# One dummy matmul becomes 21 short ones, and the written-out orders change: a two-layer linear-attention and MLP kernel

## The chip, the core and the metric

The kernel runs on one core of a Trainium2 chip. The metric is the device time of one execution in microseconds (us), the median of some runs. A core has TensorE (PE, matmuls; its weight loads are listed as PEld), VectorE (DVE), ScalarE (ACT), GpSimd (POOL) and SyncE (SP, which issues most transfers), and 16 DMA engines that all queues share.

## The reference

x has 2048 tokens of 512 values in bfloat16. Two layers run the same two blocks, with the same weights.

```
x = x + A(layernorm(x));  x = x + B(layernorm(x))      # twice
A: q, k, v = y @ wqkv, 32 heads of 16
   phi(t) = where(t > 0, t + 1, exp(t)) + 1e-6
   kv = sum over tokens of phi(k) v^T;  z = sum over tokens of phi(k)
   out = (phi(q) kv) / (phi(q) z + 1e-6) @ wo
B: gelu(layernorm(y) @ w1 + b1) @ w2 + b2              # 512 -> 1792 -> 512
```

## The kernel before

**Tiles.** Tokens come in 16 tiles of 128 (named st, 0 to 15), four to a chunk (c, 0 to 3; k is the tile within it). Every step of work on a tile is one named operation, and most are one instruction. PE's operations are groups of matmuls: four of 512 columns accumulate over the 512 inputs.

**Names.** The first digit behind the letters is the layer (0 or 1).
- Loads: x0 and x1 (first chunk of x, tile 0 and tiles 1 to 3), xc1 to xc3 (the other chunks), wka to wkd (quarters of the key weights), wq, and later wv, wo, w1, w2.
- Layernorm of a tile (`norm`, line 757): stats (L775, DVE), aggr (L777), veps (L782, POOL or DVE), pow (the reciprocal root, L784, POOL), nmr (L795, POOL, only where ACT normalises), norm (L803 on DVE, L798 on ACT). The letter A or B behind a name tells the block. Tile 3 of layer 0 takes its sums on ACT (sumA0_3, sqA0_3).
- Transposes of normalised tiles: TA, TB, and TP for phi(q), as DMA transposes issued by SP one after the other (`transpose`, L812); PTA and PTC for the first four tiles by PE (`transpose_pe`, L825), with a copy tc on ACT (L835). Tiles 0 and 1 are transposed centred only (cenA0_0, cenA0_1), and the scale is put in later.
- Attention: K (L879) and Q (L896, L909) are projections; exp and relu on ACT and min and phi on DVE or POOL make phi of them (L847 to L864); G (L984, L1013) gathers y^T phi(k) over all tokens; Z (L970), ZH and za add up z, with zs sums on DVE; KV (L1034) and M (L1057) turn G into one matrix, through the copies cpg and cpm; D (L1100), ln, rec, pr or pz, red, den, rec, pr divide by the denominator; WO (L1123) multiplies and RA (L1128) adds to x.
- MLP: W1 (L1153) with a gelu on ACT for each (L1158), W2 (L1190, L1176) with RB (L1196, L1200); the last number of W1 is the token half where the first chunk is split; b2 adds the bias row to x. OD writes the output.

**Stages.** Chunk loads and K, G, Q of layer 0 (about 5 to 48 us), attention output and MLP of layer 0 chunk by chunk, with K, G and Q of layer 1 between (to about 200 us), then the same output and MLP of layer 1.

**Dummies.** `warm` (L749) is a group of PE matmuls on a constant whose result nobody reads. `WARM` in CONF lists the columns of each; warm0 has seven matmuls of 512 columns, warm1 to warm8 one of 256 each. Each matmul has its own weight load.

**What sets the order.** `CONF` holds it, written out: `ORDER` lists for each engine its operations in sequence, `PLACES` which buffer each tile uses, `WAY` which engine runs an operation that can go to several. At build time the operations are issued in exactly this order, and `assign_waits` puts a semaphore wait before an instruction wherever its data or its buffer depends on another engine. An engine doesn't pass a waiting instruction. The numbers of expected durations in the code only decide ties of this writing out; no planner runs in the kernel.

The heads of PE's and DVE's lists are these (PE's list begins at line 254):

```
pe:  warm0 warm8 warm2 warm6 PTC0 warm1 warm7 warm5 warm4 warm3 K0_0a K0_0b PTC1 K0_0c K0_0d PTA0_2 K0_1 PTA0_3 K0_2
     K0_3 G0_0_0 G0_1_0 Q0_0_2 Q0_0_1 Q0_0_0 K0_5 G0_2_0 K0_4 Z0_0 G0_3_0 Q0_1_0 K0_7 Q0_1_3 K0_6 ...
dve: ones statsA0_0 aggrA0_0 cenA0_0 statsA0_2 statsA0_1 aggrA0_2 aggrA0_1 cenA0_1 normA0_0 vepsA0_1 normA0_2
     statsA0_5 normA0_3 aggrA0_5 normA0_1 statsA0_4 mink0_0 ...
```

Of the kernel before, what the change touches and what calls it, by code (L numbers as in the profile page):

```python
# [185 lines left out]
def assign_waits(graph, order, sems, dma_sems):  # L186
# [10 lines left out]
    while len(done) < total:  # L197
        moved = False
        for e in ENGINES:
# [42 lines left out]
    WARM=[[512, 512, 512, 512, 512, 512, 512], [256], [256], [256], [256], [256], [256], [256], [256]],  # L242
    LOADS=[['x0', 'sp', 'x', 0, 0, 1, ''], ['x1', 'sp', 'x', 0, 1, 4, ''], ['wkb', 'act', 'wk', 0, 2, 3, 'ones'], ['wka', 'sp', 'wk', 0, 0, 1, ''], ['wkd', 'act', 'wk', 0, 3, 4, ''], ['wkc', 'sp', 'wk', 0, 1, 2, ''], ['xc1', 'sp', 'x', 1, 0, 4, 'x0'], ['wq', 'sp', 'wq', 0, 0, 4, ''], ['xc3', 'sp', 'x', 3, 0, 4, ''], ['xc2', 'sp', 'x', 2, 0, 4, '']],
    ORDER={
# [39 lines left out]
        "act":  # L284
# [324 lines left out]
def build_kernel(nc, A_x, A_wqkv, A_wo, B_x, B_w1, B_b1, B_w2, B_b2, out, conf=None, report=False):  # L609
# [5 lines left out]
    with ExitStack() as es:  # L615
# [137 lines left out]
        def by_token(L, c):  # L753
            return eng(f"den{L}_{c}") == "tok"
# [605 lines left out]
```

## Time and profile before

| | |
|---|---|
| median of 3 runs | 323.07 us (322.53 to 324.76) |
| profiled execution, its time | 323.1 us |
| its span, first to last instruction | 321.9 us |
| busy: PE, DVE, ACT, POOL | 318.0, 218.1, 189.3, 145.5 us |
| matmuls (each with a weight load) | 1703 |
| instruction packets, queues q8 and q14 | 13 (0.21 MB) and 10 (0.08 MB) |

How to read it: in rows of the timeline and of the chain, the first number is the start and the second the length, in us; then the engine, the line of the kernel, what is written and read, and how often. A bracket gives the engine's idle time ahead of it and what ended it. A row of the waits gives engine, output and line, what it waited for, us in total, times, and the longest. A matmul's length in the trace has a tail of some 0.16 us that overlaps with the next; the distance of starts tells the pace. A matmul of 512 columns follows the one before by 0.216 us for most of the run.

### The profile page before, as it was taken

To read this page: it belongs to the slowest core of one execution; us is meant where nothing else is said; L and a number is where in the kernel's file an instruction comes from. 1 tells how busy PE (TensorE), PEld (TensorE's weight loads), DVE (VectorE), ACT (ScalarE), POOL (GpSimd) and SP (SyncE) were. 2 spreads that over 40 slices of the span, in tenths; PEclk is the share of its full clock that TensorE was granted. 3 is DMA by queue.
4 is the path that set the end of the run, shared out by engine and by line. 5 is a ranking of instruction groups with operands and counts; after the bars stand their busy time and mean duration, and the time that the engine had idled before them with its cause. 6 is when DMAs were issued, how large, how long until landed. Compare 5 with 4: busy or idle time off the path is not lost.

```text
span 321.9 us, 4748 instructions
## 1 busy us (share of the span) xinstructions
PE 318.0 (99%) x1703; PEld 157.4 (49%) x1703; DVE 218.1 (68%) x529; ACT 189.3 (59%) x324; POOL 145.5 (45%) x216
## 2 busy tenths in 40 slices
PE   8999999999999999999999999999999999999997
PEld 3444554666444444444444444558544444444444
DVE  5998789999786774028848899999889881101103
ACT  5898656797730636667962367979634442663320
POOL 6573978688655355101822415887454163000000
DMA  7844793142121412111010200122232322201002
GB/s 257 200 81 85 241 348 85 35 82 36 33 49 34 82 33 51 34 33 32 18 40 10 51 16 0 35 51 52 50 62 54 98 65 67 49 0 35 16 33 65
DMA packets 52355, 21.68 MB, mean 67 GB/s; under 512 B 47532, under 2 KB 50860, under 8 KB 52332
## 3 DMA queue, kind: packets, MB, share of 16 engines
q1 hardware_dynamic: 50844, 16.37, 22.4%
q0 software_dynamic: 1056, 4.72, 4.3%
q10 hardware_dynamic: 432, 0.30, 0.3%
q8 instruction: 13, 0.21, 0.3%
q14 instruction: 10, 0.08, 0.1%
HBM read 8.00 MB, written 2.10 MB: 31 GB/s over the span
## 4 chain that ended last, share of the span: by engine, by line
PE 97%; DMA 2%; DVE 0%; issue 0%
PE ps L1153 30%; PE ps L1190 29%; PE ps L1123 9%; PE ps L879 8%; PE ps L896 6%; PE ps L984 4%; PE ps L1013 4%; DMA t<-in_A_x_dram 2%; PE ps L909 2%; PE ps L1176 1%; PE ps L970 1%; PE ps L1034 1%; PE ps L1057 1%; PE ps L1100 1%; DVE stats L775 0%; PE ps L1048 0%
## 5 line engine op out<-in xcount | busy, mean ns | idle before, releaser
L1158 ACT ACTIVATE gT<-ps,b1c 128x512 bf16<-128x512 f32 (+1 forms) x140 | 77.0, 601 | 68.7 <-PE ps L1153 68.1
L1153 PE MATMUL ps<-t,w 128*128 128x512 bf16 (+1 forms) x560 | 102.5, 336 | 0.0
L1190 PE MATMUL ps<-w,gT 128*128 128x512 bf16 x434 | 98.6, 379 | 0.0
L1153 PEld LDWEIGHTS ps<-t,w 128*128 128x128 bf16 x560 | 54.8, 98 | 43.7 <-ACT gT L1158 0.2
L1190 PEld LDWEIGHTS ps<-w,gT 128*128 128x128 bf16 x434 | 42.5, 98 | 50.4
L784 POOL TENSOR_TENSOR rstd<-veps,neghalf 128x1 f32<-128x1 f32 x64 | 39.0, 625 | 41.1 <-DVE veps L782 38.9
L847 ACT ACTIVATE eb<-ps 128x512 bf16<-128x512 f32 x62 | 35.4, 606 | 19.3 <-PE ps L896 7.3
L1200 DVE TENSOR_TENSOR yb<-ps,xsb 128x512 bf16<-128x512 f32 x15 | 10.2, 688 | 41.4 <-PE ps L1190 41.4
L775 DVE BATCH_NORM_STATS2 stats<-xsb 128x6 f32<-128x512 f32 x48 | 32.0, 681 | 0.3
L1123 PE MATMUL ps<-gtb,t 128*128 128x512 bf16 x128 | 31.4, 379 | 0.0
L879 PE MATMUL ps<-wqkv,t 128*128 128x512 bf16 x128 | 30.9, 379 | 0.3 <-ACT t L835 0.3
L858 ACT ACTIVATE rb<-ps 128x512 bf16<-128x512 f32 x43 | 25.3, 607 | 5.8 <-PE ps L879 5.8
L798 ACT ACTIVATE yb<-xsb,nmr,rstd 128x512 bf16<-128x512 f32 x21 | 16.9, 814 | 15.1 <-POOL nmr L795 15.1
L896 PE MATMUL ps<-wqkv,t 128*128 128x512 bf16 x96 | 24.1, 379 | 0.0
L1089 POOL TENSOR_TENSOR t<-t,rr 128x512 bf16<-128x512 bf16 x18 | 19.3, 1072 | 9.0 <-DVE rr L1085 6.4
L782 POOL TENSOR_SCALAR veps<-mv 128x1 f32<-128x1 f32 x35 | 8.2, 236 | 32.7 <-DVE mv L777 31.3
L1196 DVE TENSOR_TENSOR xsb<-ps,xsb 128x512 f32<-128x512 f32 x16 | 10.8, 678 | 17.9 <-PE ps L1190 17.9
L1139 POOL TENSOR_TENSOR xsb<-xsb,b2b 128x512 f32<-128x512 f32 x17 | 21.4, 1267 | 3.0 <-DVE yb L803 2.9
L1077 POOL TENSOR_TENSOR lr<-t,zrow 128x512 f32<-128x512 bf16 x14 | 16.5, 1179 | 7.3 <-ACT zrow L997 4.5
L1123 PEld LDWEIGHTS ps<-gtb,t 128*128 128x128 bf16 x128 | 12.5, 98 | 14.5
L803 DVE TENSOR_SCALAR yb<-xsb,mv,rstd 128x512 bf16<-128x512 f32 x27 | 14.5, 542 | 7.3 <-POOL rstd L784 6.0
L879 PEld LDWEIGHTS ps<-wqkv,t 128*128 128x128 bf16 x128 | 12.1, 98 | 14.7 <-ACT t L835 0.9
(99 smaller groups left out, 363.7 us busy)
## 6 DMA issues: line engine op xcount, KB each, us to landing
w<-in_B_w_dram POOLq DMA_DIRECT2D x4, 896.0 KB, 9.1
out_dram<-yb SPq DMA_DIRECT2D x15, 128.0 KB, 2.0
t<-in_A_x_dram SPq DMA_DIRECT2D x3, 512.0 KB, 4.8
t<-yb SPq DMA_TRANSPOSE x62, 2.5
wqkv<-in_A_wqkv_dram SPq DMA_DIRECT2D x1, 512.0 KB, 5.9
wqkv<-in_A_wqkv_dram POOLq DMA_DIRECT2D x1, 512.0 KB, 4.7
wo<-in_A_wo_dram POOLq DMA_DIRECT2D x1, 512.0 KB, 5.3
t<-in_A_x_dram SPq DMA_DIRECT2D x1, 384.0 KB, 3.3
```

The source lines that it names most:

```text
L775: G.op("dve", lambda e: e.bn_stats(stats[:, s.slot, :], src()), 620, reads=src_keys, writes=[k + "s"], tiles=[s, *src_tiles], name=f"stats ...
L784: G.op("pool", lambda e: e.tensor_tensor(rstd[:, s.slot:s.slot + 1], veps[:, s.slot:s.slot + 1], neghalf[:], op=ALU.pow), 570, reads=[k + ...
L847: G.op("act", lambda e: e.activation(eb[:, et.slot, :], bank(bt), ACT.Exp, scale=by()), 478, reads=[src_key, *more_keys], writes=[f"e{tag} ...
L858: G.op("act", lambda e: e.activation(rb[:, rt.slot, :], bank(bt), ACT.Relu, scale=by()), 478, reads=[src_key, *more_keys], writes=[f"r{tag ...
L879: ins = e.matmul(bank(b), lhsT=yTa(yT)[:, dt, k * P:(k + 1) * P], rhs=wqkv[:, dt, D:2 * D], start=(i == 0 and n == 0), stop=(i == len(part ...
L896: ins = e.matmul(bank(b), lhsT=yTa(yT)[:, dt, k * P:(k + 1) * P], rhs=wqkv[:, dt, 0:D], start=(dt == 0), stop=(dt == DT - 1))
L1089: lambda e, d=d, tok=tok, heads=heads: e.tensor_tensor(heads(tok()), heads(tok()), rr[:, d.slot, :].unsqueeze(2).broadcast_to([P, H, DH]), ...
L1123: ins = e.matmul(bank(wb), lhsT=yTa(pq)[:, kt, k * P:(k + 1) * P], rhs=gtb[:, kt, :], start=(kt == 0), stop=(kt == DT - 1))
L1139: G.op("pool" if on_pool else "dve", lambda e: e.tensor_tensor(xsb[:, st, :], xsb[:, st, :], b2b[:], op=ALU.add), 1120 if on_pool else 600 ...
L1153: ins = e.matmul(bank(b, n), lhsT=w1[:, dt, ft * P:(ft + 1) * P], rhs=yTa(yT)[:, dt, k0 * P:k1 * P], start=(dt == 0), stop=(dt == DT - 1))
L1158: G.op("act", lambda e, ft=ft, b=b, k0=k0, k1=k1, n=n: e.activation(gT[:, g.slot, ft * 512 + k0 * P:ft * 512 + k1 * P], bank(b, n), ACT.Ge ...
L1190: ins = e.matmul(bank(b), lhsT=gT[:, g.slot, ft * 512 + k * P:ft * 512 + (k + 1) * P], rhs=w2[:, ft, :], start=(ft == 0), stop=(ft == FT - 1))
```

## The change

It has three parts.

1. The seventh matmul of warm0 (512 columns) becomes 21 of 24 columns each. PE then has 1723 matmuls. The other eight dummies stay, but only warm5 and warm6 come ahead of PTC0, and six behind it.
2. `ORDER`, `PLACES` and `WAY` are written anew. The lists of loads and the first 16 entries of SP stay as they are; most other lists are permuted, from place to place, up to about the second chunk of the last MLP.
3. The code gets options: an order of chunks for each phase (`CHUNKS`), a load of half a tile, and a "half" way for the denominator, in which two tiles of a chunk go one way and two the other. `CHUNKS` names 0 to 3 in order, and neither `LOADS` nor `WAY` names a half.

```diff
-    WARM=[[512, 512, 512, 512, 512, 512, 512], [256], [256], [256], [256], [256], [256], [256], [256]],
+    WARM=[[512, 512, 512, 512, 512, 512, 24, 24, 24, 24, 24, 24, 24, 24, 24, 24, 24, 24, 24, 24, 24, 24, 24, 24, 24, 24, 24], [256], [256], [256], [256], [256], [256], [256], [256]],
+    CHUNKS=[[0, 1, 2, 3], [0, 1, 2, 3], [0, 1, 2, 3]],
...
         "pe":
-            "warm0 warm8 warm2 warm6 PTC0 warm1 warm7 warm5 warm4 warm3 K0_0a K0_0b PTC1 K0_0c K0_0d PTA0_2 K0_1 PTA0_3 K0_2 "
-            "K0_3 G0_0_0 G0_1_0 Q0_0_2 Q0_0_1 Q0_0_0 K0_5 G0_2_0 K0_4 Z0_0 G0_3_0 Q0_1_0 K0_7 Q0_1_3 K0_6 G0_4_0 G0_5_0 "
+            "warm0 warm5 warm6 PTC0 warm8 warm1 warm3 warm4 warm2 warm7 K0_0a K0_0b K0_0c PTC1 K0_0d PTA0_2 K0_1 PTA0_3 K0_2 "
+            "K0_3 G0_0_0 G0_1_0 Q0_0_2 Q0_0_1 Q0_0_0 K0_5 G0_2_0 G0_3_0 K0_4 Q0_1_0 K0_7 Q0_1_3 Z0_0 G0_4_0 K0_6 G0_5_0 "
...
-            "W11_0_8_0 W11_0_2_0 W11_0_7_0 W11_0_1_0 W11_0_0_0 W11_0_10_0 W11_0_4_0 W11_0_9_0 W11_0_13_0 W11_0_5_0 W11_0_3_0 "
-            "W11_0_0_1 W11_0_12_1 ...
+            "W11_0_9_0 W11_0_13_0 W11_0_8_0 W11_0_7_0 W11_0_4_0 W11_0_2_0 W11_0_1_0 W11_0_12_0 W11_0_0_0 W11_0_5_0 W11_0_13_1 "
+            "W11_0_5_1 W11_0_12_1 W11_0_10_0 W11_0_10_1 ...
         "dve":
-            "ones statsA0_0 aggrA0_0 cenA0_0 statsA0_2 statsA0_1 aggrA0_2 aggrA0_1 cenA0_1 normA0_0 vepsA0_1 normA0_2 "
-            "statsA0_5 normA0_3 aggrA0_5 normA0_1 statsA0_4 mink0_0 aggrA0_4 phik0_0 mink0_1 normA0_5 phik0_1 statsA0_7 "
-            "normA0_4 aggrA0_7 mink0_2 statsA0_13 mink0_3 statsA0_6 aggrA0_13 minq0_0_2 statsA0_14 aggrA0_6 phik0_2 "
-            "statsA0_12 phik0_3 statsA0_8 normA0_6 ...
+            "ones statsA0_0 aggrA0_0 vepsA0_0 cenA0_0 statsA0_2 statsA0_1 aggrA0_2 aggrA0_1 cenA0_1 normA0_0 vepsA0_1 "
+            "normA0_2 statsA0_5 normA0_3 normA0_1 aggrA0_5 statsA0_4 mink0_0 aggrA0_4 phik0_0 mink0_1 normA0_5 phik0_1 "
+            "statsA0_7 normA0_4 aggrA0_7 statsA0_6 statsA0_12 mink0_3 statsA0_13 mink0_2 aggrA0_6 aggrA0_13 phik0_2 aggrA0_12 "
+            "statsA0_15 phik0_3 aggrA0_15 statsA0_14 minq0_0_2 mink0_5 aggrA0_14 normA0_6 ...
         "pool":
-            "id0 neghalf bdm0 bdm1 id1 vepsA0_0 powA0_0 ...
+            "id0 bdm0 b1z id1 neghalf powA0_0 ... nmrA0_10 eps6 powA0_11 bdm1 nmrA0_11 powA0_9 phik0_14 wv phik0_8 wo ...
...
     # WAY, what changes sides
-    b20_3, b20_4, b20_11, b20_13, b21_3, b21_4, pr0_0_1, pr1_2_2: pool
+    b20_3, b20_4, b20_11, b20_13, b21_3, b21_4, pr0_0_1, pr1_2_2: dve
-    b21_2, pr1_3_0, pz0_2_0, pz1_2_2, pz1_3_3: dve
+    b21_2, pr1_3_0, pz0_2_0, pz1_2_2, pz1_3_3: pool
     # and some veps and za, in both directions
...
-        def by_token(L, c):
-            return eng(f"den{L}_{c}") == "tok"
+        def by_token(L, c, k=0):
+            way = eng(f"den{L}_{c}")
+            return way == "tok" or (way == "half" and k >= 2)
+
+        def by_half(L, c):
+            return eng(f"den{L}_{c}") == "half"
...
-        for c in range(NC):
+        orders = cf["CHUNKS"]
+        for c in orders[0]:
```

More of the change, by code (lines that the diff above doesn't have):

```diff
@@ L709, in load_w, with load_half @@
                                [f"{which}_{d}" for d in range(d0, d1)], name=name, kb=128 * (d1 - d0), after=after)
+        def load_half(name, queue, h, after):
+            G.parts[("x0", 0)] = (("x0", 0, 0), ("x0", 0, 1))
+            ps_ = slice(64 * h, 64 * h + 64)
+            loaded[name] = dma(queue, lambda e: e.dma_start(
+                t4[ps_, x0[0].slot, 0:D].rearrange("p (k d) -> p k d", k=1), rows(x_dram, 0)[ps_, 0:1, :]),
+                [("x0", 0, h)], [x0[0]], name=name, kb=64, after=after)
         for name, queue, what, at, lo, hi, behind in cf["LOADS"]:
             after = [loaded[b] for b in behind.split()]
-            if what == "x":
+            if what == "half":
+                load_half(name, queue, at, after)
+            elif what == "x":
                 load_x(name, queue, at, lo, hi, after)
@@ L887, in attn_q, with fn @@
         def attn_q(L, c, yT, pq):
-            if by_token(L, c):
-                for k in range(4):
+            half = by_half(L, c)
+            own = pq
+            if half:
+                own = tokq[(L, c)] = Tile(T4, f"pqt{L}_{c}")
+            n = 2 * P if half else 4 * P
+            if not by_token(L, c):
+                for kt in range(DT):
+                    b = Tile(psum, f"q{L}_{c}_{kt}" + "c" * half, "q")
+                    def fn(e, kt=kt, b=b):
+                        for dt in range(DT):
+                            ins = e.matmul(bank(b, n), lhsT=wqkv[:, dt, kt * P:(kt + 1) * P], rhs=yTa(yT)[:, dt, 0:n],
+                                           start=(dt == 0), stop=(dt == DT - 1))
+                        return ins
+                    G.op("pe", fn, 4 * MM if n == D else 4 * (n / 2.4 + 2.5), reads=[f"yT{L}_{4 * c + k}" for k in range(n // P)] + ["wq"], writes=[f"q{L}_{c}_{kt}" + "c" * half],
+                         tiles=[b, yT], name=f"Q{L}_{c}_{kt}" + "c" * half, lat=MM_DRAIN, n=4)
+                    phi(b, f"q{L}_{c}_{kt}" + "c" * half, lambda kt=kt: yTa(pq)[:, kt, 0:n], f"pq{L}_{c}_{kt}" + "c" * half, [pq], f"q{L}_{c}_{kt}" + "c" * half, n=n)
+            for k in range(4):
+                if by_token(L, c, k):
                     b = Tile(psum, f"q{L}_{c}_{k}", "q")
@@ L900, in attn_q, with attn_z @@
                          tiles=[b, yT], name=f"Q{L}_{c}_{k}", lat=MM_DRAIN, n=4)
-                    phi(b, f"q{L}_{c}_{k}", lambda k=k: t4[:, pq.slot, k * D:(k + 1) * D], f"pq{L}_{c}_{k}", [pq],
+                    phi(b, f"q{L}_{c}_{k}", lambda k=k: t4[:, own.slot, k * D:(k + 1) * D], f"pq{L}_{c}_{k}", [own],
                         f"q{L}_{c}_{k}")
-                return
-            for kt in range(DT):
-                b = Tile(psum, f"q{L}_{c}_{kt}", "q")
-                def fn(e, kt=kt, b=b):
-                    for dt in range(DT):
-                        ins = e.matmul(bank(b), lhsT=wqkv[:, dt, kt * P:(kt + 1) * P], rhs=yTa(yT)[:, dt, :],
-                                       start=(dt == 0), stop=(dt == DT - 1))
-                    return ins
-                G.op("pe", fn, 4 * MM, reads=[f"yT{L}_{4 * c + k}" for k in range(4)] + ["wq"], writes=[f"q{L}_{c}_{kt}"],
-                     tiles=[b, yT], name=f"Q{L}_{c}_{kt}", lat=MM_DRAIN, n=4)
-                phi(b, f"q{L}_{c}_{kt}", lambda kt=kt: yTa(pq)[:, kt, :], f"pq{L}_{c}_{kt}", [pq], f"q{L}_{c}_{kt}")
         zfirst = {}
-        def attn_z(L, c, pks):
-            by_sum = [int(v) for v in (eng("zc0") or "").split()] if L == 0 else list(range(NC - 1))
+        def attn_z(L, c, pks, order):
+            by_sum = [int(v) for v in (eng("zc0") or "").split()] if L == 0 else order[:NC - 1]
+            others = [v for v in order if v not in by_sum]
             def fold(add):
@@ L973, in attn_z, with attn_g_held @@
             G.op("pe", fn, 400, reads=[f"pk{L}_{4 * c + k}" for k in range(4)] + ["onesm"], writes=[f"zc{L}_{c}"], tiles=[b, *pks], name=f"Z{L}_{c}", lat=MM_DRAIN, n=16)
-            total(b, f"zc{L}_{c}", f"zs{L}_{c}", bool(L) or c != min(v for v in range(NC) if v not in by_sum))
-            if L == 0 and by_sum and c == max(v for v in range(NC) if v not in by_sum):
+            total(b, f"zc{L}_{c}", f"zs{L}_{c}", bool(L) or c != others[0])
+            if L == 0 and by_sum and c == others[-1]:
                 fold(True)
-        def attn_g_held(L, st, k, y, ykey, pk, gb):
-            parts = [(dc,) for dc in range(DT)] if st == ST - 1 else [tuple(range(DT))]
+        def attn_g_held(L, st, k, y, ykey, pk, gb, first, last):
+            parts = [(dc,) for dc in range(DT)] if last else [tuple(range(DT))]
             for part in parts:
@@ L984, in fn @@
                         ins = e.matmul(ps[:, gb.slot + dc, :], lhsT=yb[:, y.slot, dc * P:(dc + 1) * P], rhs=pkb[:, pk.slot, :],
-                                       start=(st == 0), stop=(st == ST - 1))
+                                       start=first, stop=last)
                     return ins
                 keys = [f"g{L}_{dc}" for dc in part]
-                G.op("pe", fn, len(part) * MM, reads=[ykey, f"pk{L}_{st}"] + (keys if st else []), writes=keys,
+                G.op("pe", fn, len(part) * MM, reads=[ykey, f"pk{L}_{st}"] + ([] if first else keys), writes=keys,
                      tiles=[y, pk, gb], name=f"G{L}_{st}_{part[0]}", lat=MM_DRAIN, n=len(part))
@@ L1004, in attn_g_out, with attn_g_chunk @@
                 copy(gtb[:, dc, :], gb, f"g{L}_{dc}", ("gt", dc), dc % 2, f"g{L}_{dc}", off=dc)
-        def attn_g_chunk(L, c, ys, ykeys, pks):
+        def attn_g_chunk(L, c, ys, ykeys, pks, first, last):
             for dc in range(DT):
@@ L1042, in attn_kv @@
                  reads=["zs", "bdmask"], writes=["zb"], name=f"zb{L}", lat=40, fast=True)
-            if any(by_token(L, c) for c in range(NC)):
+            if any(by_token(L, c, 3) for c in range(NC)):
                 zr = Tile(psum, f"zr{L}", "t")
@@ new lines, in attn_den @@
+            half = by_half(L, c)
+            src = tokq[(L, c)] if half else pq
+            pt = pq if half or not by_token(L, c) else Tile(T4, f"pt{L}_{c}")
+            n = 2 * P if half else 4 * P
+            if not by_token(L, c):
+                for kt in range(DT):
+                    tag = f"{L}_{c}_{kt}" + "c" * half
+                    b = Tile(psum, f"d{tag}", "n")
+                    r = Tile(LR, f"lr{tag}")
+                    key = f"pq{L}_{c}_{kt}" + "c" * half
+                    G.op("pe", lambda e, kt=kt, b=b: e.matmul(bank(b, n), lhsT=zb[:, kt * P:(kt + 1) * P], rhs=yTa(pq)[:, kt, 0:n], start=True, stop=True),
+                         MM if n == D else n / 2.4 + 2.5, reads=[key, "zb"], writes=[f"d{tag}"], tiles=[b, pq], name=f"D{tag}", lat=MM_DRAIN)
+                    G.op("act", lambda e, b=b, r=r: e.activation(lr[:, r.slot, 0:n], bank(b, n), ACT.Ln, bias=eps6[:]), 575 if n == D else 362,
+                         reads=[f"d{tag}", "eps6"], writes=[f"l{tag}"], tiles=[b, r], name=f"ln{tag}", lat=90, table="exp")
+                    G.op("act", lambda e, r=r: e.activation(lr[:, r.slot, 0:n], lr[:, r.slot, 0:n], ACT.Exp, scale=-1.0), 536 if n == D else 323,
+                         reads=[f"l{tag}"], writes=[f"l{tag}"], tiles=[r], name=f"rec{tag}", lat=110, table="exp")
@@ L1093, in attn_den @@
[L1093 to L1105 removed]
+                         lambda e, kt=kt, r=r: e.tensor_tensor(yTa(pq)[:, kt, 0:n], yTa(pq)[:, kt, 0:n], lr[:, r.slot, 0:n], op=ALU.mult),
@@ new lines, in attn_den, with attn_out @@
+                     1150 if on_pool else 600, reads=[f"rr{tag}", f"pq{tag}"], writes=[f"pq{tag}"], tiles=[d, src],
+                     name=f"pr{tag}", lat=60, fast=not on_pool)
+                dma("sp", lambda e, k=k, tok=tok: e.dma_start_transpose(yTa(pt)[:, :, k * P:(k + 1) * P], tok()), [f"pt{tag}"],
+                    tiles=[src, pt], reads=[f"pq{tag}"], name=f"TP{tag}", sem=("pT", src, k), transpose=True)
+            return pt
+        def attn_out(L, c, k, pq, base, base_keys, base_tiles, first):
@@ L1116, in attn_out @@
             st = 4 * c + k
             wb = Tile(psum, f"wo{L}_{st}", "w")
-            parts = [(kt,) for kt in range(DT)] if st == 0 else [tuple(range(DT))]
+            parts = [(kt,) for kt in range(DT)] if first else [tuple(range(DT))]
             for part in parts:
@@ L1141, in mlp_front, with mlp_up @@
                  fast=not on_pool)
-        def mlp_up(L, c, yT, g):
-            parts = [(0, 2), (2, 4)] if c == 0 else [(0, 4)]
+        def mlp_up(L, c, yT, g, first):
+            parts = [(0, 2), (2, 4)] if first else [(0, 4)]
             for hf, (k0, k1) in enumerate(parts):
@@ L1252, in build_kernel @@
         for L in range(2):
-            nxt = []
-            for c in range(NC):
+            nxt = {}
+            chunks = orders[1 + L]
+            for c in chunks:
                 yT = Tile(T4, f"yBT{L}_{c}")
```

118 lines of the change are left out of this document (51 added, 67 removed), and 432 rows, old and new, of tables (ORDER, PLACES, WAY).

## The prediction

> **What bounds the kernel now.** I read the page's busy times first, then the chain that ended last, then the waits of TensorE (PE), then the first 12 us of the timeline.
>
> ```profile
> span 321.9 us, 4748 instructions
> PE 318.0 (99%) x1703; PEld 157.4 (49%) x1703; DVE 218.1 (68%) x529; ACT 189.3 (59%) x324; POOL 145.5 (45%) x216
> ...
> PE 97%; DMA 2%; DVE 0%; issue 0%
> ```
>
> PE is busy 318.0 of 321.9 us, and 97% of the chain is PE. The next view, PE's waits, holds every one of them; none is longer than 0.8 us:
>
> ```profile
> PE ps L749 <- PEq L1345: 0.8, 1, 0.8
> PE ps L825 <- DVE yb L803: 0.5, 1, 0.5
> PE ps L879 <- ACT t L835: 0.3, 1, 0.3
> PE ps L825 <- DVE yb L789: 0.2, 1, 0.2
> ```
>
> The chain's first rows and the timeline place these waits; all lie before 9.16 us.
>
> ```profile
> 3.24 4.83 DMA t<-in_A_x_dram
> ...
> 8.09 0.69 DVE stats L775
> 8.79 0.33 DVE yb L803
> ...
> 9.16 0.40 PE ps L825 x4
> 9.56 1.73 PE ps L879 x8
> ```
>
> The load xc1 (second chunk of x) is issued at 3.24 and lands at 8.07. VectorE (DVE) has statsA0_5, which needs it, ahead of normA0_3 in its order, so normA0_3 runs at 8.70 to 9.10, and PE starts PTA0_3 at 9.16. From there to its last matmul PE runs without a gap: 512-column matmuls follow each other every 1.73/8 = 0.216 us, and the table by windows gives PE 50.84 busy of 50.84 us from 9.16 to 60.00, and full stretches after it until 319.70. So two things can change the time: when PE gets past PTA0_3, and new gaps after it. There is no old gap after it to remove.
>
> **The sum's base.** The profiled execution took 323.1 us: span 321.9 and 1.2 around it. The median of the three timed runs is 323.07 (322.53 to 324.76), so the profiled one stands for the median. A measurement of this kernel tells about 1% (3.2 us) from no change.
>
> **The code parts.** CHUNKS lists 0 to 3 in order three times, no unit is marked "half", no load "half". The new branches then issue what the old ones did: cost 0, nothing hides it because nothing runs. The real matmuls (1688, 1703 less 15 dummies) stay the same in number and shape; the order names are permuted.
>
> **The dummies.** Before PTC0, PE has warm0 and three groups of 256; after it, five more. The weight loads' starts give the pace:
>
> ```profile
> 2.49 0.15 PEld L749 LDWEIGHTS ps<-const-bfloat16-1.0 128*128 128x128 bf16 x1 [0.28 <-issue]
> 2.91 0.15 PEld L749 LDWEIGHTS ps<-const-bfloat16-1.0 128*128 128x128 bf16 x1 [0.28 <-issue]
> ```
>
> A dummy of 512 columns takes 0.43 us here, twice the 0.216 of later; the 256s go at 0.214 until about 4.2 us, at 0.112 after PTC0. The seventh starts at 3.34. It becomes 21 of 24 columns. No row has 24 columns at the slow pace. Lower bound: 16 one-column matmuls of L970 take 0.38 us in the chain, 24 ns each, so 21 take 0.50. Upper bound: 128 columns at the slow pace, half of the 0.214 of a 256, is 0.107, so 21 take 2.25. I take twice the one-column row, 0.048, since it is the nearest: 1.01 us, against 0.43 removed: +0.58. One 256 moves behind PTC0: -0.21. So the dummies before PTC0 end at about 4.39 + 0.37 = 4.76 (bounds 4.25 and 6.0). PTC0's other condition, cenA0_0, now has vepsA0_0 ahead of it on DVE, 0.05 to 0.14 us (a L782 row on DVE lasts 0.14), so 4.6 to 4.7. PTC0 goes from 4.61 to about 4.76. ScalarE (ACT) reads it in tcC0 at 5.23, behind sumA0_3; PTC0 would end at 5.0 + 0.2, so nothing is lost. Six dummies of 0.112 follow until about 5.7, under K0_0a at 5.86. K0_0c moves ahead of PTC1; its weights wkd landed at 5.93, so it fits from 6.3 to 6.5, before PTC1 at 6.55. All of this ends before PTA0_3, which waits for xc1; LOADS and the first eleven entries of SP are unchanged. The slack: K0_1's last matmul streams until 8.53, 0.63 us before PTA0_3; on ACT expk0_0 ends at 9.22 and tcA0_3 starts at 9.59, 0.37. **Cost 0**; at the upper bound PTC0 is 1.4 late, less 0.63 to 0.37 of cover and 0.25 of moved dummies, some +0.5.
>
> The Trainium skill, "TensorE: Matmul & The Clock Gate", section "What's actually happening", says that a window of about 3.4 us of activity releases the array's clock from half rate, and that the window runs free of the kernel's start. The trace agrees in that the pace doubles 3.4 us after the first dummy at 0.83; by that rule alone the short ones change nothing if they count as activity, and the sum stays.
>
> **The instruction packets.** The page lists "q8 instruction" with 13 packets, in the trace 110 to 149 matmuls apart, so this queue brings PE's instructions. The first is at 18.05 us and takes 1.26 us. Twenty more matmuls ahead bring every later one 20 matmuls earlier: 20 x 0.216 = 4.3 us, so the first comes near 13.7. A packet costs PE nothing by itself (no gap at any of the 13). But look at the transposes' landings, page first, then the DMA view of 17 to 19 us:
>
> ```profile
> t<-yb SPq DMA_TRANSPOSE x62, 2.5
> ```
>
> ```profile
> q8 instruction: 1, 0.02, 3.9%
> issues: line engine op xcount, KB each, median us to landing
> t<-yb SPq DMA_TRANSPOSE x1, 4.1
> ```
>
> TA0_6, in flight beside the packet, took 4.05 us against 2.45: stretched by 1.6 us. It landed at 21.76, and K0_6 started at 21.89, so the stretch was just covered. Freeing TA0_6 therefore gains **0**: PE was not waiting. At 13.7 the packet meets the load xc2 (10.76 to 14.58) and TA0_5, queued behind it (11.45 to 15.14); K0_5 starts at 15.44, as it does in the new order: cover 0.29. Bounds: 0 (TA0_5's own packets run after 14.6, when a packet begun at 13.3 is through) and 1.6 - 0.29 = 1.3. PE's sequencer runs a varying distance ahead (the same 110 to 149), so the place is uncertain by a few us. I take 0, as most of TA0_5's flight is waiting for xc2, and keep 1.3.
>
> The skill, "Runtime: NRT & Kernel Launch", section "Instruction fetch mechanics", has fetch mostly hidden from the engine. By that the shift costs 0; for PE itself the trace agrees, for the transposes beside it TA0_6 does not.
>
> **The orders.** I follow the new ones by start-to-start steps of rows: a statistics 0.61 us on DVE, min 0.19, aggregate 0.09, normalise or bf16 sum 0.31, PE's groups of four 0.863. DVE's order is the old one up to aggrA0_7 at 12.71. Then statsA0_6 12.80, statsA0_12 13.41, mink0_3 14.02, statsA0_13 14.21, mink0_2 14.82, two aggregates, phik0_2 15.19, ending 15.59 (was 15.83; G0_2 is due at 16.30). Aggregate, statsA0_15, phik0_3 16.20 to 16.60; G0_3 has moved ahead of K0_4 to 17.16: cover 0.56. normA0_6 moves from 17.28 to 17.68, so TA0_6 lands at about 20.6, at 22.2 if stretched; K0_6 moves back to 22.73: cover 0.5 at least. Later tight places, in the same way: WO0_0_1 at 51.18 needs pr0_0_1, which moves from POOL to DVE behind cpm0_2 (there 49.6 to 50.3) and ends at 50.9: cover 0.2, was 0.78. W11_0_13_1, the first on the second token half in layer 1, comes 13 x 0.437 after 215.12, at 220.80; TB1_3 landed at 220.12: cover 0.68. Between 60 and 66 us and 217 and 223 us PE is 0.2 to 0.6 us behind the gelus that free its banks, as before, since the same matmuls and gelus alternate. bdm1 moves on POOL from 2.5 to about 25 us, 0.85 us, ahead of nmrA0_11; normA0_11 ran at 27.44, nmrA0_11 ended at 26.48: up to 0.1 left, then TA0_11's place in its queue at 28.93 still covers 0.6. Six b2 additions go from POOL to DVE and one back, three products with zrow from DVE to POOL: PE waits for none of them in the trace. The orders from about 248 us on are the same. **Cost 0**, with bounds of -0.5 (the lowest timed run is 0.5 under the median, so some stalls differ between executions) and +1.5 (the highest is 1.7 over).
>
> **Sum**: 323.1 + 0 + 0 + 0 = 323.1 us.
>
> **Rivals.**
> - **The packet lands on TA0_5 (slower).** Place: K0_5. Price 1.26, the packet's own time, less 0.29: 0.97, giving 324.1; 324.4 with the whole 1.6. It decides once TA0_5 lands after 15.38. For it: the stretch of TA0_6; against: TA0_5 mostly waits for xc2. Chance 0.27.
> - **Executions get steadier (faster).** Orders with wider covers (phik0_9 now ends 0.9 us before the matmul that needs its bank, Z0_2's 0.19 grows) save stalls that the profiled execution didn't have: 322.5, the lowest time. Against: the profiled execution has no such stall and takes the median. Chance 0.17.
> - **The start is late.** Slow dummies as in the upper bound, or the slow pace lasting one such stretch of 3.4 us longer, to 7.6: PTC0 from 4.8, six dummies at 0.214 to 6.6, K0_0a to K0_0c at 0.43 to 7.9, PTC1, then tcC1 and K0_1 until about 9.7, 0.5 after PTA0_3's data: 323.6. Against: the covers above, and the doubling in the trace at 4.2. Chance 0.08. (That the pace doubles at another moment in another execution is what the same page's section would have.)
> - **A stage falls out of step.** The gelu stages have 0.2 us of cover; DVE takes over POOL's work there. More than 3.2 us must come together: 327. Chance 0.05.
> - **The packets don't move**, because the sequencer waits elsewhere: 323.1, same as the forecast, counted in it.
>
> **How the numbers follow.** Forecast 0.43 (322.8 to 323.5). A gain of 1% is out of reach: PE's idle time from 4.60 to 9.16 is 4.56 less 2.4 us of real matmuls (eight of 0.216, twelve transposes of 0.058), 2.1 us in all, and xc1 pins it: faster 0.01. Slower by over 1% comes from the last stage case: 0.05. Within 1%: 0.94. The range takes in the steadier case with 0.3 for its own spread, and the packet case with the whole stretch and 0.3 more: 322.2 to 324.7.
>
> **What would show it.** PE's waits after 9.2 us: none by the forecast; one on L879 before 16 us by the packet rival. PTA0_3 near 9.16 and xc1 near 8.07. The first q8 packet near 13.7. TA0_6 landing in 2.5 us. The weight loads of L749 between 3.3 and 4.7 us give the short dummies' pace. I am wrong if a gap of PE appears at WO0_0_1, W11_0_13_1 or in the gelu stages.

## The result and the profile after

The changed kernel takes 324.41 us (median of 22 runs, 322.66 to 326.99); the kernel before takes 323.19 beside it (22 runs, 322.53 to 325.58). The ratio is 1.0038 with a 95% interval of 1.0024 to 1.0053: 1.2 us slower, inside the forecast's range and within 1%, but not the "no change" of 323.1. The profiled execution took 324.38 us, so it stands for the median.

The page of the changed kernel, busy times and chain:

```profile
span 323.1 us, 4750 instructions
PE 317.0 (98%) x1692; PEld 157.9 (49%) x1723; DVE 221.0 (68%) x534; ACT 189.8 (59%) x324; POOL 143.4 (44%) x211
...
PE 93%; DVE 3%; DMA 2%; issue 1%; ACT 1%
```

The trace lacks 31 matmul records (1692 of 1723 are there, all weight loads are), so a single step of 0.43 us between matmuls is a lost record here and no gap. DVE now holds 3% of the chain, where it held nothing. PE's waits show why:

```profile
PE ps L1151 <- DVE t L1104: 1.1, 1, 1.1
PE ps L761 <- PEq L1375: 0.8, 1, 0.8
PE ps L843 <- DVE yb L821: 0.3, 1, 0.3
PE ps L843 <- DVE yb L807: 0.2, 1, 0.2
```

The last three lie at the start, as all waits of the kernel before did (dummies, PTA0_2, PTC0). The first is new and is the longest of the kernel: L1151 is WO, L1104 the product pr. It is a gap after 9.16 us, which the kernel before didn't have. PE's timeline places it; a bracket holds the idle time ahead of the row:

```profile
50.98 0.38 PE L1151 MATMUL ps<-gtb,t 128*128 128x512 bf16 x1
52.45 0.82 PE L1151 MATMUL ps<-gtb,t 128*128 128x512 bf16 x3 [1.09 <-DVE t L1104]
```

WO0_0_0 starts at 50.98, WO0_0_1 at 52.45 instead of 51.20: 1.26 us lost. The rows of the chain that answer to those of the start:

```profile
3.27 4.55 DMA t<-in_A_x_dram
...
7.85 0.69 DVE stats L793
8.54 0.33 DVE yb L821
8.92 0.40 PE ps L843 x4
```

xc1 landed at 7.83 (8.07 before), and PTA0_3 starts at 8.92 (9.16): -0.24. A third difference lies at K0_5, 15.47, which is 6.55 us behind PTA0_3 where it was 6.28: +0.27. The profile puts this small gap down to ACT's exponential expq0_0_2, which ends at 15.45, because that came last. But K0_5's first weight load starts at 15.44, before that end, and in e2 below, with the same orders, K0_5 starts at 15.38, ahead of the end of expq0_0_2 at 15.63. What PE waited for is the transpose TA0_5: it landed at 15.33 (15.14 before), behind the load xc2, which landed at 14.77 (14.58 before). So what the start gained was lost again here.

Together 1.26 + 0.27 - 0.24 = 1.29, and the unrounded spans differ by 323.14 - 321.85 = 1.29. The whole difference of the two profiled executions is placed.

**What DVE did meanwhile.** First DVE, then POOL, in the changed kernel:

```profile
49.24 1.21 DVE L869 TENSOR_SCALAR eb<-eb 128x512 bf16<-128x512 bf16 x1
...
50.64 0.62 DVE L1023 TENSOR_SCALAR gtb<-ps 128x512 bf16<-128x512 f32 x1
51.18 1.21 DVE L1104 TENSOR_TENSOR t<-t,lr 128x512 bf16<-128x512 bf16 x1
```

```profile
49.25 1.05 POOL L1134 TENSOR_TENSOR t<-t,rr 128x512 bf16<-128x512 bf16 x1
50.79 1.05 POOL L1134 TENSOR_TENSOR t<-t,rr 128x512 bf16<-128x512 bf16 x1 [0.49 <-DVE rr L1130]
```

The row at 49.24 is minq0_2_0. It took 0.28 us in the kernel before:

```profile
50.36 0.28 DVE L851 TENSOR_SCALAR eb<-eb 128x512 bf16<-128x512 bf16 x1
```

In the changed kernel it starts within 0.01 us of POOL's product pr0_1_1 and ends at 50.45, 0.15 after that product ends at 50.30. The row at 51.18 is the moved pr0_0_1: it ends at 52.40, 0.55 after POOL's next product pr0_1_0 (50.79 to 51.85), though it needs some 0.68 in all. cpm0_2 between them, at 50.64, reads PSUM and runs beside POOL's product in 0.62. So these two DVE instructions, whose operands all lie in SBUF, stand still beside POOL's products: minq0_2_0 loses 0.93 us and pr0_0_1 0.53.

That matches a rule of the Trainium skill, "SBUF — State Buffer", section "SBUF: two separate sides": DVE and GpSimd share one pair of SBUF ports as an exclusive lock; a DVE instruction takes it when it runs in a 2-port performance mode or has two inputs in SBUF, the one that starts first keeps it for its whole instruction, and PE, ACT and DVE's own pair wait for nobody. The rows above agree for pr0_0_1, with its two SBUF inputs, and for the instruction with a PSUM source that isn't held up. minq0_2_0 has one input; that it runs in such a mode no trace here states.

From here on, the **toss** is the question which of minq0_2_0 (DVE) and pr0_1_1 (POOL) goes ahead and which is held up. Only their lengths tell it, not the starts in the rows: here DVE's row starts 0.01 us ahead of POOL's and is the one held up. They meet because the instructions ahead of both, den0_1_0 on DVE and pz0_1_2 on POOL, end together (49.33 and 49.29).

### The profile page after: what moved, and what is told of

Read it like the earlier page. It is cut to its first block, busy times and chain, and to the rows that moved or that the text cites. A ratio compares the mean times of both kernels' runs of the same rounds, so it can differ in the third digit from the quotient of the medians.

```text
span 323.1 us, 4750 instructions
## 1 busy us (share of the span) xinstructions
PE 317.0 (98%) x1692; PEld 157.9 (49%) x1723; DVE 221.0 (68%) x534; ACT 189.8 (59%) x324; POOL 143.4 (44%) x211
## 4 chain that ended last, share of the span: by engine, by line
PE 93%; DVE 3%; DMA 2%; issue 1%; ACT 1%
PE ps L1181 30%; PE ps L1218 29%; PE ps L1151 8%; PE ps L897 8%; PE ps L930 5%; PE ps L1036 4%; PE ps L1007 4%; DMA t<-in_A_x_dram 2%; PE ps L918 2%; PE ps L1204 1%; DVE gtb L1023 1%; PE ps L993 1%; DVE rd L1125 0%; DVE t L1104 0%; DVE eb L869 0%
## 5 line engine op out<-in xcount | busy, mean ns | idle before, releaser
L1181 PE MATMUL ps<-t,w 128*128 128x512 bf16 (+1 forms) x552 | 101.9, 336 | 0.4
L1181 PEld LDWEIGHTS ps<-t,w 128*128 128x128 bf16 x560 | 54.8, 98 | 43.7 <-ACT gT L1186 0.6
L802 POOL TENSOR_TENSOR rstd<-veps,neghalf 128x1 f32<-128x1 f32 x64 | 41.2, 659 | 23.1 <-DVE veps L800 21.3
L1151 PE MATMUL ps<-gtb,t 128*128 128x512 bf16 x124 | 31.3, 379 | 1.3 <-DVE t L1104 1.1
L897 PE MATMUL ps<-wqkv,t 128*128 128x512 bf16 x125 | 30.6, 379 | 0.3
L1122 POOL TENSOR_TENSOR lr<-t,zrow 128x512 f32<-128x512 bf16 x17 | 19.7, 1160 | 9.9 <-ACT zrow L1020 4.7
L1151 PEld LDWEIGHTS ps<-gtb,t 128*128 128x128 bf16 x128 | 12.4, 98 | 15.8 <-DVE t L1104 1.6
L897 PEld LDWEIGHTS ps<-wqkv,t 128*128 128x128 bf16 x128 | 12.2, 98 | 15.0 <-ACT t L853 0.6
L981 POOL TENSOR_TENSOR zacc<-zacc,pkb 128x512 f32<-128x512 f32 x5 | 6.2, 1243 | 28.9 <-DVE mv L795 19.6
L821 DVE TENSOR_SCALAR yb<-xsb,mv,rstd 128x512 bf16<-128x512 f32 x27 | 15.2, 568 | 3.2 <-POOL rstd L802 2.9
```

The source lines that it names most:

```text
L802: G.op("pool", lambda e: e.tensor_tensor(rstd[:, s.slot:s.slot + 1], veps[:, s.slot:s.slot + 1], neghalf[:], op=ALU.pow), 570, reads=[k + ...
L897: ins = e.matmul(bank(b), lhsT=yTa(yT)[:, dt, k * P:(k + 1) * P], rhs=wqkv[:, dt, D:2 * D], start=(i == 0 and n == 0), stop=(i == len(part ...
L1122: lambda e, r=r, tok=tok: e.tensor_tensor(lr[:, r.slot, :], tok(), zrow[:], op=ALU.mult), 1150 if on_pool else 600,
L1151: ins = e.matmul(bank(wb), lhsT=yTa(pq)[:, kt, k * P:(k + 1) * P], rhs=gtb[:, kt, :], start=(kt == 0), stop=(kt == DT - 1))
L1181: ins = e.matmul(bank(b, n), lhsT=w1[:, dt, ft * P:(ft + 1) * P], rhs=yTa(yT)[:, dt, k0 * P:k1 * P], start=(dt == 0), stop=(dt == DT - 1))
```

## The experiments

Each label is one kernel. The runs of one chip share the runs of the kernel before there: e1 to e4 (before: 323.47, 35 runs), e5 to e8 (323.04, 35 runs), e9 to e12 (323.62, 29 runs). Each was timed 12 times, e11 6 times. The ratios and intervals are as recorded; a ratio is not exactly the quotient of the two medians. In e1, e5, e9 and e11 an edited order list stands on one line, so their line numbers are lower than those of the changed kernel.

**e1_product_on_pool**: the product back on POOL.

```diff
 "pool": ... pz0_1_2
+        pr0_0_1
         pr0_1_1 pr0_1_0 ...
 "dve":  ... cpm0_2
-        pr0_0_1
         red0_1_2 ...
 "act":  ... expq0_2_0
-        cpm0_0 rec0_0_1
+        rec0_0_1 cpm0_0
-    "pr0_0_1": "dve"
+    "pr0_0_1": "pool"
```

> The new orders and dummies, but pr0_0_1 goes back from DVE to POOL, ahead of pr0_1_1, and rec0_0_1 goes back ahead of cpm0_0 on ACT. In the changed kernel's profile PE waits 1.26 us at WO0_0_1 for pr0_0_1, which DVE finishes at 52.40. Theory (DVE's place for pr0_0_1, beside POOL's products): the wait at WO0_0_1 goes, 323.2 (323.0 to 323.6), 1.0 to 1.4 under the changed kernel. Rival (the 21 short dummies and the packets that they move): unchanged, 324.4. Rival (the new orders as a whole, at many places): between 324.0 and 324.4.

Measured: 323.39 (322.81 to 324.84), ratio 1.0012 [0.9994, 1.0029]. minq0_2_0 took 0.28, and the wait at WO0_0_1 is gone. But the profiled execution, 324.41 us, has other waits:

```profile
PE ps L1094 <- DMA t<-yb: 0.9, 1, 0.9
PE ps L674 <- PEq L1288: 0.8, 1, 0.8
PE ps L810 <- ACT t L766: 0.8, 1, 0.8
```

L1094 is W1, the first matmul of the MLP near 60.5 us, which waits for TB0_1: issued at 57.76, landed at 61.72, 3.96 us instead of 2.5, beside an instruction packet of q8 at 59.71. L810 is K0_0a at the start. What follows: this price can be taken away, and there are two more, which the profile of the changed kernel did not show.

**e2_old_dummies**, and again **e7_old_dummies_again**: all orders of the change, with the old warm0.

```diff
-    WARM=[[512, 512, 512, 512, 512, 512, 24, ... 24], [256], ...
+    WARM=[[512, 512, 512, 512, 512, 512, 512], [256], ...
```

> The new orders, but warm0 with its seven matmuls of 512 columns again. Theory: the wait at WO0_0_1 stays at 1.0 to 1.3 us, 324.3 (323.9 to 324.6). Rival (packets): the first q8 packet goes back towards 21 us by the orders' matmuls, PE's wait at K0_5 goes, 323.2.

> The new orders with the old warm0 once more, beside the changed kernel on one chip. Theory A: the same mixture as the changed kernel, within 0.4 us. Theory B: 323.3, 1.1 below it.

Measured: 323.33 (322.75 to 324.90), ratio 0.9999 [0.9983, 1.0016]; and 323.31 (322.97 to 325.19), ratio 1.001 [0.9993, 1.0028]. In both profiles DVE won the toss. DVE and POOL in e2:

```profile
49.16 0.28 DVE L869 TENSOR_SCALAR eb<-eb 128x512 bf16<-128x512 bf16 x1
...
50.17 0.73 DVE L1104 TENSOR_TENSOR t<-t,lr 128x512 bf16<-128x512 bf16 x1
50.83 0.67 DVE L1125 TENSOR_REDUCE rd<-lr 128x32 f32<-128x512 f32 x1
```

```profile
49.16 2.66 POOL L1134 TENSOR_TENSOR t<-t,rr 128x512 bf16<-128x512 bf16 x2
```

The two start at the same 49.16 as printed. minq0_2_0 takes its 0.28, pr0_0_1 runs from 50.17 to 50.90, which is the end that the prediction had, and WO follows without a gap. POOL is held up in its place (1.20 and 1.50 for its two products, 1.05 alone), and nobody waits for it. The sum at 50.83 also reads SBUF alone and keeps its 0.67 beside POOL's second product (50.32 to 51.82), so not every DVE instruction on SBUF operands is held up. So the new orders cost nothing when DVE wins. The expectation of e2 had the wait at WO0_0_1 stay, with 324.3; that missed. Its rival's 323.2 came, but by the toss: the first packet came at 18.82 and not near 21 us. Whether the old dummies make DVE win, or whether it merely did in these two profiles, stays open.

**e3_short_dummies_alone**: the kernel before with the new warm0.

```diff
-    WARM=[[512, 512, 512, 512, 512, 512, 512], [256], ...
+    WARM=[[512, 512, 512, 512, 512, 512, 24, ... 24], [256], ...
```

> The kernel before, with the new warm0 alone (six of 512 and 21 of 24 columns). Theory: the short dummies and the packets cost nothing that can be measured, 323.2 (322.8 to 323.6), PE without waits behind PTA0_3. Rival (packets): 324.0 to 324.4, with PE waiting at K0_5 for TA0_5.

Measured: 323.35 (322.55 to 324.73), ratio 0.9999 [0.9983, 1.0015]. The page's only wait of PE is the old one of the dummies. The first q8 packet came at 17.36 (18.05 before), the third at 57.13, where it stretched TB0_0 to 3.99 us (55.24 to 59.23) without a gap on PE. The short dummies alone cost nothing that can be measured.

**e4_small_products_on_pool**: POOL's two products shortened.

```diff
+                hn = 1 if tag in ("0_1_1", "0_1_0") else H
...
-                         heads(tok()), heads(tok()), rr[:, d.slot, :] ...
+                         heads(tok())[:, 0:hn, :], heads(tok())[:, 0:hn, :], rr[:, d.slot, 0:hn] ...
```

> The changed kernel, but POOL's pr0_1_1 and pr0_1_0 divide 16 of 512 columns; the division of the other 496 columns of two token tiles is left out. Nothing on DVE is changed. Theory (a DVE instruction of this kind waits for the end of a long POOL instruction): minq0_2_0 falls from 1.21 us to 0.28, pr0_0_1 from 1.21 to 0.69, pr0_0_1 ends at 50.9 and the wait at WO0_0_1 goes, 323.2. Rival (the instructions are slow for another reason, or DVE's sequence as such is too long): their lengths stay at 1.2, and the time at 324.4.

Measured: 323.22 (322.61 to 323.80), ratio 0.9995 [0.9982, 1.0009]. pr0_1_1 took 0.35, minq0_2_0 0.28, pr0_0_1 0.67. No run is above 323.80, while 18 of the 22 first runs of the changed kernel, timed apart from these, are at 323.96 or above. With POOL out of the way, short dummies and new orders together cost nothing measurable. It leaves out work of POOL, though, so e10 below repeats it with all of the work.

**e5_product_on_dve_alone**: the kernel before, with pr0_0_1 moved to DVE.

```diff
 "pool": ... pz0_1_2
-        pr0_0_1
         pr0_1_1 ...
 "dve":  ... cpm0_2
+        pr0_0_1
         red0_1_2 ...
```

> The kernel before, with pr0_0_1 alone moved from POOL to DVE, right behind cpm0_2; dummies and all else as before. Here pr0_1_1 on POOL must wait for rec0_1_1, which DVE makes only after pr0_0_1, so POOL runs no product beside it. Theory (it is the POOL instruction in flight that costs, not pr0_0_1 on DVE): pr0_0_1 takes 0.7 us, ends at 50.1, no wait at WO0_0_1, 323.3 (322.9 to 323.7). Rival (the move to DVE costs by itself): 324 and more.

Measured: 323.52 (323.00 to 323.99), ratio 1.0007 [0.9996, 1.0018]. DVE's row:

```profile
49.14 0.68 DVE L1052 TENSOR_TENSOR t<-t,lr 128x512 bf16<-128x512 bf16 x1
```

Here DVE has no den and no min ahead of the product, so it runs at 49.14, 0.68 long, and ends 1.1 us ahead of WO0_0_1 (50.93). So the move of the product costs nothing by itself, where no product of POOL runs beside it.

**e6_changed_again**: the changed kernel, on another chip.

> The changed kernel once more, on the chip of the next two. In its profile den0_1_0 on DVE and pz0_1_2 on POOL end together at 49.3, and then minq0_2_0 (DVE) and pr0_1_1 (POOL) start within 0.01 us of each other; minq0_2_0 lost and took 1.21 us. With the old dummies it started at the same place, won, and took 0.28. Theory A (a toss that each execution makes anew): times in two groups some 1.2 us apart, as many of each here as with the old dummies, medians within 0.4 of each other. Theory B (the short dummies decide the toss): 324.4 here, 323.3 with the old dummies.

Measured: 323.89 (323.01 to 325.91), ratio 1.0024 [1.0005, 1.0042]: the loss is there again. The profiled execution happens to be the longest, and DVE won the toss (minq0_2_0 0.28):

```profile
PE ps L897 <- ACT t L853: 1.1, 1, 1.1
PE ps L1181 <- DMA t<-yb: 1.1, 1, 1.1
```

These are the two waits of e1: K0_0a (L897) at the start, and W1 (L1181) for TB0_1, which took 4.18 us beside a packet at 61.08. So the toss is one price of three.

**e8_four_dummies_of_128**: the same 512 columns in fewer pieces, so 3 matmuls more instead of 20.

```diff
-    WARM=[[512, 512, 512, 512, 512, 512, 24, ... 24], [256], ...
+    WARM=[[512, 512, 512, 512, 512, 512, 128, 128, 128, 128], [256], ...
```

> The new orders, the seventh dummy made of four matmuls of 128 columns: the same columns, 3 instead of 20 matmuls more, so the packets move by 0.6 us instead of 4.3. Theory A: like the other two. Theory B with the packets as the cause: 323.3, like the old dummies. Theory B with short dummies as such as the cause: 324.4.

Measured: 323.19 (322.72 to 325.10), ratio 1.0003 [0.9985, 1.0022]. DVE won the toss; a wait of 0.4 at W1 for TB0_0 and TB0_1, stretched to 4.31 and 3.49 by a packet at 57.68. The three kernels with the new orders but fewer dummy matmuls (e2, e7, e8) are all the same as before within their intervals. Neither theory of e6 to e8 came out: the changed kernel's median is 0.58 and 0.70 us above e7's and e8's on this chip, where A had at most 0.4 and B 1.1, and the times of all three spread over more than 2 us, so their order isn't certain.

**e9_gap_on_dve** and **e11_gap_and_old_dummies** settle the toss for POOL: a memset of 0.07 us on DVE, ahead of minq0_2_0. e9 is the changed kernel, e11 the same with the old dummies.

```diff
+        scr = SB("scr", [P, 16], FP32)
...
+        G.op("dve", lambda e: e.memset(scr[:], 0.0), 60, writes=["scr"], name="gap")
...
 "dve":  ... den0_1_0
+        gap
         minq0_2_0 ...
```

> The changed kernel, with one more VectorE instruction, a memset of 16 unused columns, ahead of minq0_2_0, so that POOL's product pr0_1_1 starts first. The toss theory: minq0_2_0 takes 1.2 us instead of 0.28 in the profile, pr0_0_1 ends beside pr0_1_0 near 52.4, WO0_0_1 waits 1.2 us, and this in nearly every run: median 324.3 to 324.6, most runs above 323.9. The rival, that the packets and the start make the spread and the toss is one price among several: median 323.9 to 324.2, as the changed kernel on the second chip had 323.89.

> The orders of the change with the old dummies, and the same memset ahead of minq0_2_0. If the toss alone prices the change and the dummies only sway it: minq0_2_0 1.2 us, WO0_0_1 waits 1.2, median 324.3 to 324.6, as with the short dummies. If the price needs the short dummies (through their packets or the start): 323.3, as the orders with the old dummies had.

Measured: e9 324.60 (323.99 to 325.95), ratio 1.0036 [1.0021, 1.005]; e11 325.06 (324.51 to 325.22), ratio 1.0043 [1.0028, 1.0057]. Every run of both is above 323.98. POOL's product, DVE and the wait in e9:

```profile
48.59 1.06 POOL L1093 TENSOR_TENSOR t<-t,rr 128x512 bf16<-128x512 bf16 x1
48.61 1.19 DVE L828 TENSOR_SCALAR eb<-eb 128x512 bf16<-128x512 bf16 x1
...
50.52 1.21 DVE L1063 TENSOR_TENSOR t<-t,lr 128x512 bf16<-128x512 bf16 x1
```

```profile
PE ps L1110 <- DVE t L1063: 1.1, 1, 1.1
```

With the memset ahead of it, minq0_2_0's row starts 0.02 us behind POOL's, and WO0_0_1 comes 1.26 us late, in e9 as in e11. The old dummies don't protect the orders: once POOL is first, the price is the same. The expectation of 324.3 to 324.6 had the 323.2 of the kernel before in mind, 1.1 to 1.4 us more; on this chip that kernel is at 323.62, and the differences are 1.0 and 1.4 us.

**e10_pool_waits_for_dve** settles it for DVE, with all of the work kept: pr0_1_1 waits for pr0_0_1.

```diff
+        pair = {o.name: o for o in G.ops}
+        pair["pr0_1_1"].deps[pair["pr0_0_1"]] = True
```

> The changed kernel, all of its work kept, but POOL's product pr0_1_1 waits until VectorE's pr0_0_1 has ended, so that the two engines cannot meet at minq0_2_0 or at pr0_0_1; 21 short dummies and all orders stay. pr0_1_1 then runs from about 51.0 to 52.1, pr0_1_0 behind it. The toss theory: minq0_2_0 0.28 us, pr0_0_1 0.68, no wait at WO0_0_1, median 323.2 with at most two runs of twelve above 323.9, as with the products of 16 columns. The rival, that the short dummies' packets cost the rest: median 323.6 to 324 and a third or more of the runs above 323.9, from W1's wait for TB0_1 near 60 us.

Measured: 323.74 (322.81 to 324.96), ratio 1.0004 [0.999, 1.0018]: no loss left that can be measured. minq0_2_0 took 0.28, pr0_0_1 0.67. Five of twelve runs are above 323.9, where at most two were expected, and the median lies in the rival's 323.6 to 324, though the kernel before is at 323.62 on this chip; so the toss is not all that spreads the runs. The rival named W1's wait; in the profiled execution (324.06) that gap is 0.23, and most of the loss against e2's profile is at the start:

```profile
PE ps L897 <- ACT t L853: 1.2, 1, 1.2
```

**e12_changed_third**: the changed kernel beside these three.

> The changed kernel once more, beside the other three on one chip. A mixture of runs that lose the toss (324.4) and runs that win it (323.2): the median between 323.5 and 324.5, a third to four fifths of the runs above 323.9. It should lie between the two kernels in which the toss is settled.

Measured: 323.99 (322.49 to 326.05), ratio 1.0019 [0.9999, 1.004], 6 of 12 runs above 323.9. Its median lies between that of the kernel in which POOL is first (324.60) and that of the one in which DVE is (323.74), as a mixture would. But its twelve runs spread over 3.6 us, and it is clear of neither of the two, nor of the kernel before. In its profiled execution DVE won the toss, and the two other waits are there:

```profile
PE ps L897 <- ACT t L853: 1.1, 1, 1.1
PE ps L1181 <- DMA t<-yb: 0.9, 1, 0.9
```

Their causes are in two more views. The first holds ACT's first row in the changed kernel's own trace, the second that of e12:

```profile
4.70 0.63 ACT L784 ACTIVATE eb<-t 128x512 bf16<-128x512 bf16 x1 [2.62 <-DMA t<-in_A_x_dram]
```

```profile
5.55 0.63 ACT L784 ACTIVATE eb<-t 128x512 bf16<-128x512 bf16 x1 [3.48 <-DMA t<-in_A_x_dram]
```

This is sumA0_3, which needs the load x1. ACT's order has it ahead of tcC0, the copy that K0_0a waits for. x1 landed at 5.53 us in e12, against 4.67 in the changed kernel's trace. PTA0_3 then starts at 9.47, 0.5 late. The other wait, by the DMA view of e12 from 57.9 to 61 us, in which only TB0_1 is issued (at 57.93):

```profile
q8 instruction: 1, 0.02, 1.9%
issues: line engine op xcount, KB each, median us to landing
t<-yb SPq DMA_TRANSPOSE x1, 4.0
```

One instruction packet, at 59.85, and the transpose beside it takes 4.0 us instead of 2.5. It lands at 61.95; the gap at W1 is 1.07.

**The three prices together**, from the profiled executions of all kernels with 21 short dummies and the new orders. An asterisk marks a toss that the kernel itself settles or makes harmless.

| profiled | time, us | toss won by | x1 landed | third q8 packet | TB0_1 issued, landed | gaps of PE, us |
|---|---|---|---|---|---|---|
| changed | 324.38 | POOL | 4.67 | 55.43 | 58.75, 61.22 | WO0_0_1 1.26, K0_5 0.27 |
| e1 | 324.41 | DVE* | 5.35 | 59.71 | 57.76, 61.72 | W1 1.02, start 0.4 |
| e4 | 322.72 | DVE* | 4.45 | 53.66 | 57.09, 59.55 | none |
| e6 | 325.91 | DVE | 5.62 | 61.08 | 59.05, 63.23 | W1 1.23, start 1.8 |
| e9 | 323.99 | POOL* | 4.41 | 56.16 | 58.81, 61.30 | WO0_0_1 1.26, W1 0.26 |
| e10 | 324.06 | DVE* | 5.62 | 54.52 | 58.70, 61.19 | start 0.6, W1 0.23 |
| e12 | 324.77 | DVE | 5.53 | 59.85 | 57.93, 61.95 | W1 1.07, start 0.5 |

"Start" is how much later PTA0_3 starts than in e2 (8.93 us). In e6 the slow pace also came back. The dummies near 5 us ran at the fast one (256 columns every 0.11 us); after the wait at K0_0a, 128 columns took 0.107 us from 8.13 to 9.31 and 512 columns 0.43 at 9.86, twice the usual, and the granted clock over the first 10 us was 0.85, where it was 1.00 in the changed kernel's first profile and in e12. That makes its start the worst. The sum works about: e12's span is 1.5 us longer than e2's (323.5 against 322.0), and its gaps are 1.07 + 0.5 = 1.6.

In the seven other profiled executions (before, e2, e3, e5, e7, e8, e11) x1 landed between 4.46 and 4.70. PE's gaps ahead of a W1 are 0.58 us at most there (e7 and e11 near 79 us, for TB0_4, stretched to 3.97 by a packet; e8 0.54 and e5 0.47 near 60 us). So the third price is not the short dummies' alone: with fewer dummy matmuls a packet stretched TB0_1 too, for a smaller gap.

## Why the prediction was right and wrong

- **The bound and the start**: right. PE sets the end, xc1 and PTA0_3 the start (7.83 and 8.92). The range holds the result, and so does "within 1%", but the range by luck: its upper end, 324.7, was set by the packet case, and what came is another mechanism of about that size. The forecast itself, no change, is off by 1.2 us. The prediction named a gap at WO0_0_1 as a sign of being wrong, and that gap came.
- **The code parts, cost 0**: right as far as the runs tell. e2 and e7 hold all of them and show no loss.
- **The dummies, cost 0**: right in the profile, with one term mis-sized. The 21 took 0.61 us (3.34 to 3.95), 29 ns each, between the one-column row (24) and my 48; PTC0 started at 4.70 (forecast 4.76). In e3 they cost nothing by themselves that can be measured.
- **The instruction packets**: the step "so the first comes near 13.7" failed. It came at 16.91 us, 1.1 earlier instead of 4.3, and the second at 38.16 (38.13 before). The third to fifth did come 4.1 to 4.8 earlier (55.43, 73.10 and 96.20, against 59.56, 77.86 and 100.50). In the kernels with 21 short dummies the first came between 16.57 and 20.46 and the third between 53.66 and 61.08, so one packet can't be placed to within a few us. TA0_6 landed in 2.39 us as forecast, and TA0_7 was stretched in its stead (14.99 to 19.03), still 0.7 us ahead of K0_7. The packet rival had the right place and the wrong cause: K0_5 did wait for TA0_5, 0.27 us, but no packet was near; TA0_5 came behind xc2, and PE was 0.24 us earlier. Where a packet costs PE something is TB0_1 near 60 us, by the third packet, at 1.0 to 1.2 us (e1, e6, e12). That the rival's 0.97 is near this size is chance.
- **The orders, cost 0**: this is the step that failed. "WO0_0_1 at 51.18 needs pr0_0_1, which moves from POOL to DVE behind cpm0_2 (there 49.6 to 50.3) and ends at 50.9: cover 0.2." In e2 every number of it holds (cpm0_2 49.63 to 50.25, the product's end 50.90). In the changed kernel's profile the product ends at 52.40. I took DVE's durations from rows that POOL did not disturb, and didn't look at what POOL does in the same microsecond: two products of 1.05 us each, while DVE has a min and a product there whose operands all lie in SBUF. The trace of before held the warning: five DVE instructions on SBUF operands in it last 1.02 to 1.64 us, where most rows of the same lines last 0.28 or 0.69; the one of 1.64, at 75.18, lies beside POOL's additions of the bias, which run from 74.67 to 80.09. A cover of 0.2 against stretches of 0.93 and 0.53 us, which is what the two instructions lost, is no cover, and it deserved a rival of its own.
- **The rivals**: "executions get steadier" is refuted; they get less steady (322.49 to 326.05 in e12, 322.88 to 324.69 in the kernel before beside it). "The start is late" is seen in four profiles of kernels with the change (e1, e6, e10, e12), by another cause than the one given, x1 landing at 5.35 to 5.62 instead of 4.41 to 4.70; in e6 the slow pace came on top, but as one that came back after the wait and not as one that lasted. It isn't in the changed kernel's own profile. "A stage out of step" did not occur: W11_0_13_1 and the gelu stages show no gap.

**What is shown and what stays open.** Shown: POOL first at minq0_2_0 costs 1.26 us at WO0_0_1 (the changed kernel's profile, and e9 and e11 at will), DVE first costs nothing there (e2, e7, e10), and with the toss settled for DVE the change makes no difference that can be measured (e10, 1.0004; 0.86 us under e9). Short dummies alone (e3) and the orders with fewer dummies (e2, e7, e8) are the same as before within their intervals. Not shown: that the loss of the changed kernel's median needs both parts, since its runs and those of e7 and e8 overlap, and that the toss makes up most of that loss, since e10 and e12 differ by 0.25 us with runs that overlap too. Open: whether and how the 20 additional matmuls sway the toss and bring x1 late. x1 is issued at 1.24 or 1.25 us in all kernels, and it lands late in four of the seven profiles of the table against none of the other seven. That may be an effect of the longer program or chance in single profiles. How many executions of the changed kernel lose the toss is not known either: only profiled executions show it, one of three lost it, and the times alone (18 of 22, 6 of 12 and 6 of 12 runs above 323.9) mix the three prices.

## What to carry to other kernels

When an instruction moves from GpSimd to VectorE, look at what GpSimd runs in the same microsecond: for a bf16 product or min with all operands in SBUF, like the two here, price the move with GpSimd's whole instruction as a possible delay, not with the undisturbed duration. Two such instructions on the two engines whose predecessors end together make a tight place into a toss, and a wait that settles it (e10) cost nothing that can be measured where the other engine had room. A wait that the profile puts down to the last of several releases may have ended by another (K0_5). A profile is one draw: where the times spread over more than the effect, several profiles of the same kernel tell more than one.

## What was unexpected

- Two rows that start within 0.01 us of each other end in two ways, 1.26 us apart, and the rows don't tell which: in the changed kernel's profile DVE's row is 0.01 us ahead (49.24 and 49.25) and is held up, in e12's it is as much ahead (49.69 and 49.70) and is not. A memset of 0.07 us was enough to settle it in the profiles of e9 and e11, and every run of both is above 323.98.
- A held-up instruction can lose several times its own length: minq0_2_0, 0.28 us of work, took 1.21 beside a product of POOL of 1.05. In the other direction POOL's products went from 1.05 to 1.20 and 1.50 (e2).
- An instruction packet of 16 KB stretches the DMA transpose beside it from 2.5 to about 4.0 us, and the next one in the queue when both are in flight. It is the transposes that carry this to PE: each gap ahead of a W1 of more than 0.5 us follows the landing of a stretched one. The Trainium skill, "Runtime: NRT & Kernel Launch", section "Instruction fetch mechanics", calls the cost of a new block mostly hidden; for PE's sequencer that agrees, since no gap lies at a packet itself, but W1's 1.07 us in e12 came by way of the transpose beside it.
